# Attention, expert routing and two MLPs on one core: queries' high parts by DMA, gates through the routing matmuls

## The chip, the cores and the metric

The kernel runs on one core of a Trainium2 chip. Its metric is device time in microseconds (us). Three runs of the kernel before took 915.15, 915.86 and 917.76 us; the median is 915.86 us.

Five engines work side by side, each through its own list of instructions in a fixed order: TensorE (PE; its weight loads are PEld), VectorE (DVE), ScalarE (ACT), GpSimd (POOL) and SyncE (SP), which here only issues DMAs. An engine that waits holds up all that stands behind it in its list.

## The reference

Three layers in fp32: attention with a decay (4 batches, 8 heads, 576 rows, 64 columns), a mixture of 8 experts, and an MLP with a rational function.

```
cum    = cumsum(log(clip(f, 1e-4, 1)))                  # per head, along the 576 rows
scores = q @ k.T / 8 + cum[i] - cum[j], masked above the diagonal
attn   = exp(scores - rowmax);  attn /= attn.sum() + 1e-9
x      = attn @ v                                       # 2304 x 512 over batches and heads
logits = x @ w_gate;  e = argmax(logits)                # 8 experts
gate   = softmax(logits)[e] * sigmoid(x @ w_output_gate)[e]
y      = gate * (relu(x @ w1[e]) @ w2[e])               # 512 -> 1024 -> 512
h      = y @ w_in                                       # 512 -> 2048
out    = (P(h) / Q(h)) @ w_out                          # P cubic, Q from |h| and h*h
```

## The kernel before

Accuracy comes from splits: a number is a high part, rounded to the type that TensorE takes in one pass, and a low part, the rest. A product is three matmuls (high by high, low by high, high by low); in the scores two matmuls do it, since a second operand holds queries' high parts and rows of ones beside the low parts and the decay.

**Attention (to 198 us of the trace).** Sixteen pairs of heads are worked through, four to a batch. For each pair:

- SP loads keys `rk` and queries `rq` (64 rows of each head of the pair, 288 KB each), values `v`, and the two decay rows into `kl` (`load_c`, L387). These rows come from `cum_d` in DRAM, which the start of the kernel writes (L337) after a log (ACT L310), a running sum (DVE L314) and a split (L328, L332).
- The splits: `kh` (keys' high parts, DVE L410, two casts of 128x576 a pair), `kl` (low parts, POOL L415), `qs` high (ACT L421), `qs` low (POOL L424) and `q2s` (the copy of queries' high parts, POOL L429, function `q2h`). For the first pair DVE does the low parts and copies.
- Scores on PE (L455, L456; the last 64 rows L466, L467); the row minimum with the mask on DVE (L478, L490, function `least`); the exponential with its row sum on ACT (L510, L521); PE transposes (L573 to L593); ACT or DVE move them out of PSUM (L290, L292); the product with the values (L616) and its move out (`ot`).

After a batch's four pairs come its batch operations: sums of the last rows (`tails`, L672, L680), 1e-9 and reciprocal of the sums (`norm`, L690, L691), logits (L699 to L724), one-hot choice of the expert (`choose`, L739 to L744), the gate (`gates_a` L750 to L752, exponentials on ACT L755 and L756, `gates_b` L760 to L769), and the rows x scaled by 1/sum and gate (`rows_m` L785 on DVE, or `rows_c` L794 on ACT and `rows_g` on POOL), written to DRAM as `x_d` (L805).

The order of all that is not written by hand. `Plan` (L58) is given each operation with the engines that can do it and their lengths in ns, what it needs, buffers that it takes and frees, and a due time (`when`, in units of a pair, from the numbers `T_...`). It simulates the engines: of the operations that could begin soonest on an engine (within `NEAR` ns) it takes the one with the smallest due time; `DEAR` is a handicap of an engine where two could do the work. The result is issued in that order, and each engine keeps it.

**Routing (198 to 220 us).** With the last batch's choice, matmuls count tokens by expert (`ptot`, `pcnt`), DVE makes running sums, slots and places (L944 to L1000: counts, `ceil_div` L918 and L919, one-hot tables `so`, `rs`, `op_`), and 20 matmuls (`pid`, L1005) give each slot of an expert's tile the number of its token (`ids`, L1007). POOL gathers rows of `x_d` by `ids` (L1144). Beside it POOL scales the last batch's rows, and ACT makes the high parts of the first expert's weights (`split_unit`, L1035), DVE the low parts (L1037).

**Experts and MLP (220 us to the end).** For each of the slots' tiles: transposes (L1163), split (`hi_lo`, ACT L1063 and DVE L1064), three matmuls for each product (`mm3`, L1169 to L1171), output `ys` by ACT (L1193) to DRAM. Then the rational MLP (L1378 to L1429), which PE fills.

The lines that the change touches most, in the kernel before: the casts of the keys are DVE's alone, and the queries' second copy is POOL's.

```python
nc.vector.tensor_copy(d["kh"][:, h], d["rk"][:, h])
...
return lambda e: (nc.vector if e == "DVE" else nc.gpsimd).tensor_scalar(
    q2[half[h], h, 0:S], d["rq"][half[h], h], 1.0, 1.0, op0=ALU.mult, op1=ALU.mult
)
```

## Time and profile before

| what | value |
|---|---|
| median of three runs | 915.86 us |
| the profiled execution | 916.76 us |
| its span, first to last instruction | 915.0 us |
| PE busy | 868.4 us, 95% |
| DVE busy | 742.2 us, 81% |
| ACT busy | 619.1 us, 68% |
| POOL busy | 339.6 us, 37% |
| mean granted TensorE clock | 0.985 |

The profile is of one execution, 0.90 us above the median. 1.76 us of it lie outside the span. Busy shares are averages over stages with different limits: the stage, not the total, tells what an engine's work is worth. The clock column gives TensorE's clock as a share of its full 2.4 GHz; 0.50 is 1.2 GHz.

The span in 40 slices of 22.9 us (busy tenths) shows where PE is not full: the first slice, the seventh to ninth (137 to 206 us), and the tenth (206 to 229 us).

```
PE   6999998976799999999999999999999999999996
DVE  7798999778676689788864899989898888989873
POOL 7788595534212213223121124243332324324223
```

### The profile page before, as it was taken

Reading aid. Unit: us, or ns where it says so; the run is one execution under the profiler, and the core shown is the slowest. Engines: PE = TensorE matmul, PEld = TensorE weight load, DVE = VectorE, ACT = ScalarE, POOL = GpSimd, SP = SyncE. Lnnn points to the kernel's source line nnn. Section 1 sums busy time; section 2 is a strip of 40 time slices with the busy share of each in tenths; the row PEclk is TensorE's granted clock in tenths of the full one; section 3 lists DMA queues with packets and bytes.
Section 4 is the critical chain, followed back from the end, with each engine's and each line's share of the span. In section 5 each row is a group of like instructions: output and inputs, shape, how many; then the busy total and the mean of one; then the engine's idle time right before and its main releaser. Section 6 shows DMA issues by size and latency. Waiting matters only on the chain. (4 is left out here: it accounts for less than half of the span.)

```text
span 915.0 us, 14857 instructions
## 1 busy us (share of the span) xinstructions
PE 868.4 (95%) x4733; PEld 720.1 (79%) x4733; DVE 742.2 (81%) x1395; ACT 619.1 (68%) x1261; POOL 339.6 (37%) x356
## 2 busy tenths in 40 slices
PE   6999998976799999999999999999999999999996
PEld 5787786754688888788887778889888889988885
DVE  7798999778676689788864899989898888989873
ACT  4889887773364567666643787877676667777664
POOL 7788595534212213223121124243332324324223
PEclk9999999997999999999999999999999999999999
DMA  6675567415755378878743312011000001000001
GB/s 173 153 203 159 159 183 209 144 53 179 253 179 196 103 265 290 294 255 300 238 150 108 124 61 66 1 47 27 20 35 13 24 0 47 24 1 35 1 1 46
DMA packets 50147, 110.25 MB, mean 120 GB/s; under 512 B 8405, under 2 KB 12526, under 8 KB 50062
## 3 DMA queue, kind: packets, MB, share of 16 engines
q1 hardware_dynamic: 39214, 74.09, 26.4%
q0 software_dynamic: 10848, 35.14, 11.3%
q8 instruction: 39, 0.64, 0.3%
q14 instruction: 46, 0.38, 0.1%
HBM read 151.79 MB, written 20.35 MB: 188 GB/s over the span
## 5 line engine op out<-in xcount | busy, mean ns | idle before, releaser
L1409 POOL TENSOR_TENSOR gl<-raw,gh 128x512 fp32r<-128x512 f32 (+1 forms) x80 | 95.8, 1199 | 242.7 <-ACT gh L1408 150.2
L1425 PE MATMUL pa<-wu,gl 128*128 128x512 f32 x288 | 113.0, 392 | 1.1 <-POOL gl L1409 1.1
L1423 PE MATMUL pa<-wu,gh 128*128 128x512 f32 x288 | 113.7, 395 | 0.0
L1424 PE MATMUL pa<-wu,gh 128*128 128x512 f32 x288 | 112.6, 391 | 0.0
L1388 ACT ACTIVATE raw<-ph 128x512 f32<-128x512 f32 (+1 forms) x80 | 44.3, 553 | 80.1 <-PE ph L1380 76.8
L1064 DVE TENSOR_TENSOR colAl<-px,colAh 128x512 fp32r<-128x512 f32 x70 | 47.9, 687 | 48.7 <-ACTq L1075 25.3
L1037 DVE TENSOR_TENSOR wu<-raw,wu 128x1024 fp32r<-128x1024 f32 x64 | 75.4, 1221 | 8.4 <-ACT wu L1035 8.0
L510 ACT ACTIVATE pr<-t,mn 128x384 f32<-128x384 f32 (+3 forms) x128 | 70.6, 555 | 16.1 <-DVE mn L478 15.6
L1391 DVE SCALAR_TENSOR_TENSOR raw<-raw,babs 128x512 f32<-128x512 f32 (+1 forms) x80 | 60.8, 761 | 24.3 <-ACT raw L1389 23.8
L1401 DVE SCALAR_TENSOR_TENSOR raw<-raw,coef,raw 128x512 f32<-128x512 f32 (+1 forms) x80 | 66.0, 825 | 17.4 <-ACT raw L1397 14.4
L1378 PE MATMUL ph<-colAh,wi 128*128 128x512 f32 x192 | 74.9, 390 | 0.8 <-ACTq L1319 0.8
L1379 PE MATMUL ph<-colAl,wi 128*128 128x512 f32 x192 | 74.8, 390 | 0.2 <-DVEq L1319 0.2
L1380 PE MATMUL ph<-colAh,wi 128*128 128x512 f32 x192 | 74.7, 389 | 0.0
L1169 PE MATMUL ph<-wu,colAh 128*128 128x512 f32 x176 | 73.8, 420 | 0.7 <-ACT colAh L1063 0.7
L1169 PE MATMUL py<-wu,colAh 128*128 128x512 f32 x176 | 70.9, 403 | 1.3 <-ACT colAh L1063 1.3
L1171 PE MATMUL ph<-wu,colAl 128*128 128x512 f32 x176 | 69.8, 396 | 0.0
L1170 PE MATMUL ph<-wu,colAh 128*128 128x512 f32 x176 | 69.6, 396 | 0.0
L1171 PE MATMUL py<-wu,colAl 128*128 128x512 f32 x176 | 69.0, 392 | 0.2 <-DVE colAl L1064 0.2
L1170 PE MATMUL py<-wu,colAh 128*128 128x512 f32 x176 | 68.7, 391 | 0.0
L1063 ACT ACTIVATE colAh<-px 128x512 fp32r<-128x512 f32 x70 | 41.6, 596 | 37.4 <-PE px L1184 26.1
L1035 ACT ACTIVATE wu<-raw 128x1024 fp32r<-128x1024 f32 x64 | 63.8, 1053 | 3.2 <-DMA raw<-in_w_dram 2.8
L1425 PEld LDWEIGHTS pa<-wu,gl 128*128 128x128 f32 x288 | 54.0, 188 | 14.0 <-POOL gl L1409 2.4
(236 smaller groups left out, 2428.7 us busy)
## 6 DMA issues: line engine op xcount, KB each, us to landing
raw<-in_w_dram SPq DMA_DIRECT2D x92, 1024.0 KB
rk<-in_kT_dram SPq DMA_DIRECT2D x30, 288.0 KB
rq<-in_qT_dram SPq DMA_DIRECT2D x30, 288.0 KB
d<-in_w_in_dram POOLq DMA_DIRECT2D x16, 512.0 KB, 3.9
d<-in_w_out_dram POOLq DMA_DIRECT2D x16, 512.0 KB, 5.6
y_d<-ys SPq DMA_DIRECT2D x22, 256.0 KB
v<-in_v_dram SPq DMA_DIRECT2D x16, 256.0 KB
wo_d<-d SPq DMA_DIRECT2D x16, 256.0 KB
```

The source lines that it names most:

```text
L510: nc.scalar.activation(u["pr"][:, sl], u["t"][:, sl], AF.Exp, bias=u["mn"][:, m : m + 1], scale=-1.0, accum_out=sm[:, i, 2 * hp + h : 2 * ...
L1037: nc.vector.tensor_tensor(w[:, 1], r, w[:, 0].bitcast(F32), ALU.subtract)
L1169: nc.tensor.matmul(ps, hi[:, c, :], w[:, 0, c, :], start=start and c == 0, stop=False)
L1170: nc.tensor.matmul(ps, hi[:, c, :], w[:, 1, c, :], start=False, stop=False)
L1171: nc.tensor.matmul(ps, lo[:, c, :], w[:, 0, c, :], start=False, stop=stop and c == KD - 1)
L1378: nc.tensor.matmul(out_, wh, hi[:, :, c], start=(c == 0), stop=False)
L1379: nc.tensor.matmul(out_, wh, lo[:, :, c], start=False, stop=False)
L1380: nc.tensor.matmul(out_, wl_, hi[:, :, c], start=False, stop=(c == KD - 1))
L1409: nc.gpsimd.tensor_tensor(d["gl"], d["u_"], d["gh"].bitcast(F32), ALU.subtract)
L1423: nc.tensor.matmul(a_, gh[:, sl], wh, start=(m == 0), stop=False)
L1424: nc.tensor.matmul(a_, gh[:, sl], wl_, start=False, stop=False)
L1425: nc.tensor.matmul(a_, gl[:, sl], wh, start=False, stop=(m == MF - 1))
```

## The change

- **Plan.** New numbers `T_...`, `DEAR` and `NEAR`; a DMA's assumed latency on SP or ACT's queue is 2000 ns instead of 1000.
- **Start.** POOL's constants (zeros, ones, masks, identity) become operations of the plan, and one zeroing goes to DVE. The decay rows stay in SBUF, in a weight buffer (`cc`), instead of a trip through `cum_d`; the first pair's queries and decay rows are loaded on ACT's DMA queue.
- **Splits.** From the second pair on, `q2s` is a DMA from `qs` after its high parts are made, on SP, 30 of 147 KB, instead of 30 instructions of POOL. Casts `kh` may go to DVE or POOL, and in the first two pairs to DVE or ACT: by the order, 20 on DVE, 8 on POOL, 4 on ACT. Low parts of the first two pairs may go to DVE.
- **Batch operations.** The adds of 1e-9, the subtraction before the exponential, the gate's adds and product and the product of the gate with 1/sum go to POOL; DVE keeps a reduction (now L814) and the reciprocal (L824). The third batch's choice and gate come after the last pair.
- **Routing.** The last batch's rows are scaled by 1/sum alone, on ACT, in 40 pieces of 64 columns (L855). Its gates are not in the rows: after `ids`, five fp32 matmuls of one-hot products (`of`, L1070, by `og`) carry them to the slots (`gate`, L1076), and `ys` is scaled by it. For the other batches the same entry is 1, from the second half of `rs`, in the matmuls of `pid` (50 columns instead of 25). The rounding-up divisions become additions of a rounding constant.
- **Behind `ids`.** The low parts of the second weight unit come behind the first transposes.

The core of the diff:

```diff
-        T_BATCH, T_BATCHJ, T_ROWS = 0.299, 0.239, -5.772
...
+        T_BATCH, T_BATCHJ, T_ROWS = 0.27699, 0.20059, -5.2485
...
-        def f_store(i, t):
-            return lambda e: nc.sync.dma_start(out=cum_d[:, i, :], in_=g0[t].bitcast(F32))
...
             def load_c(e):
                 for h in range(2):
                     r = half[1 - h].start
-                    nc.sync.dma_start(out=kls[p % 2][r : r + 2, h, :].bitcast(F32), in_=cum_d[2 * p + h])
+                    queue[e].dma_start(
+                        out=kls[p % 2][r : r + 2, h, :].bitcast(F32), in_=cc[2 * p + h : 2 * p + h + 1].bitcast(F32)
+                    )
             lk, lq = {}, {}
...
+                q_ = plan.op(tl, {"SP" if p else "AQ": n}, load("rq", qT, h0, h1), takes=["rq"] if h0 == 0 else [])
                 for h in range(h0, h1):
...
+            l_c = plan.op(tl + 0.3 * SPAN, {"SP" if p else "AQ": 1200}, load_c, [o_cl, o_k[p] if p < 2 else None], takes=["c"])
...
-                    nc.vector.tensor_copy(d["kh"][:, h], d["rk"][:, h])
+                    if e == "ACT":
+                        nc.scalar.activation(d["kh"][:, h], d["rk"][:, h], AF.Copy)
+                    else:
+                        (nc.vector if e == "DVE" else nc.gpsimd).tensor_copy(d["kh"][:, h], d["rk"][:, h])
                 return go
...
             def q2h(h):
+                if p:
+                    return lambda e: nc.sync.dma_start(
+                        out=q2[half[h], h, 0:S].bitcast(F32), in_=q[half[h], h, 0:S].bitcast(F32)
+                    )
                 return lambda e: (nc.vector if e == "DVE" else nc.gpsimd).tensor_scalar(
                     q2[half[h], h, 0:S], d["rq"][half[h], h], 1.0, 1.0, op0=ALU.mult, op1=ALU.mult
...
+                khe, kle, qle, q2e = {"DVE": 520, "POOL": 1450}, {"POOL": 1480}, {"POOL": 1490}, {"SP": 1250}
+                if p < 2:
+                    khe = {"DVE": 520, "ACT": 700}
+                    kle["DVE"] = qle["DVE"] = 760
+                if p == 0:
+                    q2e = {"DVE": 850, "POOL": 1400}
+                blank_k, blank_q = (o_k[p], o_b[p]) if p < 2 else (None, None)
...
-                q2e = {"POOL": 1340} if p else {"DVE": 400}
-                o_kl.append(plan.op(w + 2, kle, kl(h), [o_kh[h]], frees=[("rk", lk[0])]))
...
-                o_q2.append(plan.op(w + 4, q2e, q2h(h), [lq[h]] + o_q2[:1], takes=["q2"] if h == 0 else [], frees=[("rq", lq[0])]))
+                o_q2.append(plan.op(w + 4, q2e, q2h(h), [o_qh[h] if p else lq[h], blank_q] + o_q2[:1], takes=["q2"] if h == 0 else [], frees=[] if p else [("rq", lq[0])]))
...
+                at = [x for x in ((slice(0, P), slice(i0, full)), (slice(0, TL), slice(NQ, i1))) if x[1].start < x[1].stop]
+                def norm_a(e, at=at):
+                    for x in at:
+                        nc.gpsimd.tensor_scalar_add(g["sums"][x], g["sums"][x], 1.0e-9)
+                def norm(e, at=at):
+                    for x in at:
+                        nc.vector.reciprocal(g["rc"][x], g["sums"][x])
+                o_n = plan.op(wn(), {"POOL": 150 * len(at)}, norm_a, need + ready + [o_mk])
+                o_n = plan.op(wn(), {"DVE": 220 * len(at)}, norm, [o_n])
+                norms.append(o_n)
                 x = {}
...
+            def gates_e(e=None):
+                nc.gpsimd.tensor_tensor(g["ex"], g["lgb"][:, :, 0:NE], g["lmax"].unsqueeze(2).to_broadcast(SH), ALU.subtract)
...
+            def gates_c(e=None):
+                nc.vector.tensor_reduce(g["den"], g["ex"], AX.X, ALU.add)
+            def gates_p(e=None):
+                den, oz = g["den"], g["oz"]
+                nc.gpsimd.tensor_scalar_add(den, den, 1.0e-9)
+                nc.gpsimd.tensor_scalar_add(oz, oz, 1.0)
+                nc.gpsimd.tensor_tensor(den, den, oz, ALU.mult)
+            def gates_r(e=None):
+                nc.vector.reciprocal(g["den"], g["den"])
+            def gates_m(e=None):
                 for r in ((slice(0, P), slice(0, NQ)), (slice(0, TL), slice(NQ, NI))):
-                    nc.vector.tensor_tensor(
-                        g["rg"][r[0], r[1], :], g["rc"][r[0], r[1], :],
-                        den[r[0], r[1]].unsqueeze(2).to_broadcast([r[0].stop, r[1].stop - r[1].start, H]), ALU.mult,
+                    nc.gpsimd.tensor_tensor(
+                        g["rg"][r], g["rc"][r], g["den"][r].unsqueeze(2).to_broadcast([r[0].stop, r[1].stop - r[1].start, H]),
...
+            def rows_a(i, y, xr):
+                np_ = P if i < NQ else TL
+                y["xr"] = xr
+                for h in range(H):
+                    sl = slice(h * D, (h + 1) * D)
+                    nc.scalar.activation(xr[:np_, sl], y["pt"][:np_, sl], AF.Identity, scale=g["rc"][:np_, i, h : h + 1])
...
+        def rows_out(i):
...
-            rows_g(i, last_y[i])
+            rows_a(i, last_y[i], wt("pr" if i < 3 else "t")[:, :DM])
...
+        nc.vector.tensor_scalar(cnt, cnt, HALF, ROUND, op0=ALU.add, op1=ALU.add)
+        nc.vector.scalar_tensor_tensor(nsl, cnt, ROUND, few, ALU.subtract, ALU.max)
+        nc.vector.tensor_tensor_scan(
+            out=send, data0=nsl, data1=zero[:, :NE], initial=0.0, op0=ALU.add, op1=ALU.add
+        )
+        nc.vector.scalar_tensor_tensor(ahead, cume[:, 0:NE], HALF, send0[:, 0:NE], ALU.add, ALU.subtract)
...
-        sidx = t_([P, NCOL], F16, name="sidx")
-        ceil_div(sidx, pos, -(P - 1) / 2)
+        sidx = t_([P, NCOL], name="sidx")
+        nc.vector.tensor_scalar_add(sidx, pos, ROUND)
         pp = t_([P, NCOL], name="pp")
-        nc.vector.scalar_tensor_tensor(pp, sidx, -float(P), pos, ALU.mult, ALU.add)
+        nc.vector.scalar_tensor_tensor(pp, sidx, ROUND, pos, ALU.subtract, ALU.subtract)
         SS = [P, NCOL, NSLOT]
-        so, rs = t_(SS, F16, name="so"), t_(SS, F16, name="rs")
...
             for c in range(c0, c0 + NI):
-                nc.tensor.matmul(pid[:, :NSLOT], op_[:, c], rs[:, c], start=(c == 0), stop=(c == NCOL - 1))
+                n = 2 if c < LAST else 1
+                nc.tensor.matmul(
+                    pid[:, : n * NSLOT], op_[:, c], rs[:, c, :n].rearrange("p a s -> p (a s)"),
+                    start=(c == 0), stop=(c == NCOL - 1), skip_group_check=True,
+                )
         ids = const.tile([P, NSLOT], I32, name="ids")
         nc.vector.tensor_scalar_add(ids, pid[:, :NSLOT], float(NT // 2))
+        den = gates_b()
+        og = t_([P, NI, NSLOT], name="og")
+        nc.vector.tensor_tensor(og, so[:, LAST:], den.unsqueeze(2).to_broadcast([P, NI, NSLOT]), ALU.mult)
+        of = ptp.tile([P, 2, NI, S], F32, tag="pT", name="of").rearrange("p h i s -> p (h i s)")[:, : NI * P]
+        of = of.rearrange("p (c q) -> p c q", q=P)
+        nc.scalar.activation(of, op_[:, LAST:], AF.Copy)
+        for i in range(NI):
+            nc.tensor.matmul(
+                pid[:, NSLOT : 2 * NSLOT], of[:, i], og[:, i], start=False, stop=(i == NI - 1), skip_group_check=True
+            )
+        gate = const.tile([P, NSLOT], F32, name="gate")
+        nc.scalar.activation(gate, pid[:, NSLOT : 2 * NSLOT], AF.Copy)
     wu_p = ctx.enter_context(tc.tile_pool(name="wu", bufs=1, reuse_waits="tile"))
...
-                nc.scalar.activation(ys, yp.pop(s), AF.Copy)
+                nc.scalar.activation(ys, yp.pop(s), AF.Identity, scale=gate[:, s : s + 1])
...
         split_unit(0, hi=False)
+        trans_x(0, col_of(0))
         split_unit(1, hi=False)
```

DVE's list at the gates of the second batch (`den` is the gate's denominator, `t` and `mn` the masked scores and their minimum, `rg` the rows' factor). Before:

```order
L752 TENSOR_REDUCE oz<-gs 128x5
L292 COPY ot<-po 128x320
L410 CAST kh<-rk 128x576
L760 TENSOR_REDUCE den<-ex 128x5
L762 TENSOR_SCALAR den<-den 128x5
L764 SCALAR_TENSOR_TENSOR den<-oz,den 128x5
L766 RECIPROCAL den<-den 128x5
L769 TENSOR_TENSOR rg<-rc,den 128x32
L769 TENSOR_TENSOR rg<-rc,den 64x8
L478 ISA t,mn<-s,mask 128x384
```

And now:

```order
L814 TENSOR_REDUCE den<-ex 128x5
L442 CAST kh<-rk 128x576
L518 ISA t,mn<-s,mask 128x512
L518 ISA mn 128x1
L442 CAST kh<-rk 128x576
L281 COPY ot<-po 128x320
L824 RECIPROCAL den<-den 128x5
```

Six instructions in a row become two that stand apart, with a row minimum (L518, L478 before), two casts and a copy between them.

The other half of that chain is now in POOL's list (L447 makes `kl`, L456 `qs` low, L819 to L828 the gate):

```order
L447 TENSOR_TENSOR kl_108<-rk,kh 64x576 x2
L456 TENSOR_TENSOR qs_104<-rq,qs_104 64x576 x2
L819 TENSOR_SCALAR den<-den 128x5
L820 TENSOR_SCALAR oz<-oz 128x5
L821 TENSOR_TENSOR den<-den,oz 128x5
L447 TENSOR_TENSOR kl_107<-rk,kh 64x576 x2
L828 TENSOR_TENSOR rg<-rc,den 128x32
L828 TENSOR_TENSOR rg<-rc,den 64x8
```

So DVE's reciprocal waits for POOL's L821, which stands behind four splits.

ACT's list at the end of routing, before (`pr`, `t`: rows of the last batch; `wu` from `raw`: high parts of the first weights; `colAh`: the first gathered rows):

```order
L755 ACTIVATE ex<-ex 128x40
L756 ACTIVATE oz<-oz 128x5
L794 ACTIVATE t<-s 64x512
L1035 ACTIVATE wu_3323<-raw_82 128x1024 x2
L1035 ACTIVATE wu_3324<-raw_83 128x1024 x2
L1035 ACTIVATE wu_3325<-raw_84 128x1024 x2
L1035 ACTIVATE wu_3326<-raw_85 128x1024 x2
L1063 ACTIVATE colAh<-px 128x512
```

And now:

```order
L855 ACTIVATE pr<-pt,rc 128x64 x15
L855 ACTIVATE t<-s,rc 64x64 x5
L803 ACTIVATE oz<-oz 128x5
L1070 ACTIVATE of<-op__3300 128x640
L1076 ACTIVATE gate<-pid 128x25
L1104 ACTIVATE wu_3354<-raw_77 128x1024 x2
L1104 ACTIVATE wu_3355<-raw_78 128x1024 x2
L1104 ACTIVATE wu_3356<-raw_79 128x1024 x2
L1104 ACTIVATE wu_3357<-raw_80 128x1024 x2
L1132 ACTIVATE colAh<-px 128x512
```

The eight weight instructions now stand behind `of`, which reads the last one-hot table, and `gate`, which reads the result of the five added matmuls.

## Rows read from the trace of the kernel before

**Rows 1.** Windows: stretch, its length, busy us (instructions) by engine, PEclk, DMA share, GB/s.

```profile
13.50:30.00 16.50, 13.36 (x76) 10.73 (x78) 10.37 (x34) 10.26 (x31) 10.11 (x21) 0.79 1.01 240
30.00:187.50 157.50, 148.48 (x1215) 120.70 (x1213) 142.63 (x477) 134.04 (x422) 108.47 (x107) 1.00 0.60 165
60.00:70.00 10.00, 10.00 (x84) 8.36 (x82) 9.27 (x34) 9.36 (x32) 9.52 (x9) 1.00 1.01 248
187.50:198.25 10.75, 10.46 (x104) 8.18 (x101) 5.94 (x28) 7.22 (x20) 2.66 (x3) 1.00 0.07 26
198.25:214.20 15.95, 3.77 (x43) 2.77 (x41) 13.86 (x38) 10.97 (x17) 8.21 (x9) 0.72 0.38 132
214.20:220.20 6.00, 4.72 (x15) 1.64 (x13) 4.67 (x5) 0.60 (x1) 4.81 (x3) 0.61 0.28 76
220.20:915.00 694.80, 680.26 (x3213) 568.98 (x3213) 555.16 (x805) 451.84 (x767) 192.96 (x185) 1.00 0.32 109
```

**Rows 2.** Timeline of the start: start, length, instruction, idle time before and releaser.

```profile
13.52 0.41 PE L456 MATMUL s<-kl,q2s 128*128 128x384 f32 x1 [4.19 <-DMA kl<-cum_d]
14.22 0.55 DVE L478 CUSTOM_DVE_ANT_0 t<-s,mask 128x384 f32<-128x384 f32 x1
```

**Rows 3.** Windows of one us each, columns as in Rows 1.

```profile
15.00:16.00 1.00, 1.00 (x6) 1.00 (x6) 0.87 (x4) 1.00 (x3) 0.18 (x2) 0.50 1.00 267
206.00:207.00 1.00, 0.00 (x0) 0.00 (x0) 0.97 (x2) 1.00 (x3) 1.00 (x2) 0.50 0.69 262
```

**Rows 4.** Timeline, 139 to 145 us.

```profile
140.58 0.26 ACT L290 ACTIVATE pT<-pt 128x128 f32<-128x128 f32 x1
142.41 1.39 POOL L424 TENSOR_TENSOR qs<-rq,qs 64x576 fp32r<-64x576 f32 x1
142.47 1.36 DVE L764 SCALAR_TENSOR_TENSOR den<-oz,den 128x5 f32<-128x5 f32 x1
144.88 0.40 PE L466 MATMUL s<-kh,qs 128*128 128x288 f32 x1 [2.60 <-DVE mn L478]
```

**Rows 5.** Lines of DVE and POOL by form, to 198.3 us: busy, mean ns, idle before.

```profile
L410 DVE CAST kh<-rk 128x576 fp32r<-128x576 f32 x32 | 21.0, 676 | 0.8 <-DMA rk<-in_kT_dram 0.8
L690 DVE TENSOR_SCALAR sums<-sums 64x8 f32<-64x8 f32 x4 | 2.9, 716 | 0.0
L764 DVE SCALAR_TENSOR_TENSOR den<-oz,den 128x5 f32<-128x5 f32 x3 | 2.7, 905 | 0.3
L429 POOL TENSOR_SCALAR q2s<-rq 64x576 fp32r<-64x576 f32 x30 | 20.3, 678 | 2.0
```

**Rows 6.** Timeline of DVE in routing.

```profile
202.63 0.20 DVE L760 TENSOR_REDUCE den<-ex 128x5 f32<-128x40 f32 x1 [1.12 <-ACT ex L755]
203.28 0.17 DVE L764 SCALAR_TENSOR_TENSOR den<-oz,den 128x5 f32<-128x5 f32 x1
204.37 1.05 DVE L979 TENSOR_TENSOR pos<-pos,oh 128x160 f32<-128x160 f32 x1
206.39 0.96 DVE L918 TENSOR_SCALAR quot<-pos 128x20 f32<-128x20 f32 x1
208.39 0.97 DVE L988 SCALAR_TENSOR_TENSOR pp<-sidx,pos 128x20 f32<-128x20 f16 x1
214.00 0.19 DVE L1007 TENSOR_SCALAR ids<-pid 128x25 int32<-128x25 f32 x1 [0.40 <-PE pid L1005]
```

**Rows 7.** Timeline of POOL, ACT and PE in routing.

```profile
204.04 3.28 POOL L785 TENSOR_TENSOR pr<-pr,rg 128x512 f32<-128x512 f32 x3 [1.42 <-DVE rg L769]
203.07 7.68 ACT L1035 ACTIVATE wu<-raw 128x1024 fp32r<-128x1024 f32 x8
213.81 4.43 PE L1256 MATMUL ph<-h 128*128 128x512 bf16 x10
219.53 0.60 ACT L1063 ACTIVATE colAh<-px 128x512 fp32r<-128x512 f32 x1 [8.79 <-PE px L1163]
220.18 0.50 PE L1169 MATMUL ph<-wu,colAh 128*128 128x512 f32 x1 [0.69 <-ACT colAh L1063]
```

More of the change, by code (lines that the diff above doesn't have):

```diff
@@ L34 @@
 }
-DEAR = {"ACT": 45.9, "DVE": 316.0}
-NEAR = 108.2
+DEAR = {"ACT": 55.495, "DVE": 310.925}
+NEAR = 14.997
 WARM = 6830
@@ L53, in reaches @@
     def reaches(self, engine):
[L54 removed]
+        lat = 2000 if self.engine in ("SP", "AQ") else LATENCY.get((self.engine, engine), 200)
         return self.end + lat
@@ L295, in evac_len, with c_blank, go, c_keys @@
             return {"ACT": 60 + 0.836 * n, "DVE": 85 + 1.04 * n}
+        queue = {"SP": nc.sync, "AQ": nc.scalar}
+        early = -4 * SPAN
+        def c_blank(i):
+            def go(e):
+                nc.gpsimd.memset(q2s[i].bitcast(F32), 0.0)
+                for h in range(2):
+                    nc.gpsimd.memset(q2s[i].bitcast(F32)[half[1 - h].start : half[1 - h].start + 2, h, 0:S], 1.0)
+            return go
+        def c_keys(i):
+            return lambda e: (nc.vector if e == "DVE" else nc.gpsimd).memset(kls[i].bitcast(F32), 0.0)
+        def c_masks(e):
+            nc.gpsimd.memset(mask, 0.0)
+            nc.gpsimd.memset(mask_t, 0.0)
+            for t in [mask[:, (NQ - 1) * P :]] + [mask_t[h * TL : (h + 1) * TL, S // 2 - TL :] for h in range(2)]:
+                nc.gpsimd.affine_select(
+                    out=t, in_=t, compare_op=ALU.is_ge, fill=BIG / SCALE, base=0, pattern=[[-1, t.shape[-1]]],
+                    channel_multiplier=1,
+                )
+        def c_gaps(e):
+            for t in qs:
+                nc.gpsimd.memset(t.bitcast(F32)[:, :, S:], 0.0)
+            make_identity(nc, identf)
+        def c_rest(e):
+            for t in vs:
+                nc.gpsimd.memset(t[: P - TL, :, NQ], 0.0)
+            nc.gpsimd.iota(
+                pref, pattern=[[-1, NE]], base=NE, channel_multiplier=0, allow_small_or_imprecise_dtypes=True
+            )
+            nc.gpsimd.tensor_copy(prefs, pref.unsqueeze(1).to_broadcast([P, NI, NE]))
+            nc.gpsimd.memset(prefs[TL:, NQ], 0.0)
+        o_k = [plan.op(early, {"DVE": 1050}, c_keys(0))]
+        o_b = [plan.op(early, {"POOL": 3200}, c_blank(0))]
+        o_m = plan.op(early + 2, {"POOL": 2300}, c_masks, o_b[:1])
+        o_g = plan.op(early + 3, {"POOL": 1300}, c_gaps, [o_m])
+        o_k.append(plan.op(early + 4, {"POOL": 1100}, c_keys(1), [o_g]))
+        o_b.append(plan.op(early + 4, {"POOL": 2700}, c_blank(1), [o_g]))
+        o_r = plan.op(early + 5, {"POOL": 1800}, c_rest, [o_b[1]])
         g0 = {}
@@ L685, in batch @@
                     need = [plan.op(wn(), {"DVE": 150}, tails2, [a2], frees=[("pt", a2)])]
-                def norm(e, i0=i0, i1=i1, full=full):
-                    for rs_, sl in ((slice(0, P), slice(i0, full)), (slice(0, TL), slice(NQ, i1))):
-                        if sl.start < sl.stop:
-                            nc.vector.tensor_scalar_add(g["sums"][rs_, sl, :], g["sums"][rs_, sl, :], 1.0e-9)
-                            nc.vector.reciprocal(g["rc"][rs_, sl, :], g["sums"][rs_, sl, :])
-                o_n = plan.op(wn(), {"DVE": 250 * (2 if i1 == NI else 1)}, norm, need + ready + [o_mk])
+                at = [x for x in ((slice(0, P), slice(i0, full)), (slice(0, TL), slice(NQ, i1))) if x[1].start < x[1].stop]
[8 more added lines that the diff above has]
+                norms.append(o_n)
                 x = {}
@@ L910, in tile_attention_moe_mlp @@
         nc.gpsimd.memset(zero, 0.0)
+        few = t_([P, NE], name="few")
+        nc.gpsimd.memset(few, 0.0)
+        nc.gpsimd.memset(few[:, 0:1], 1.0)
         SH = [P, NE, NCOL]
[L913 to L924 removed]
+        for i in range(2):
+            rows_out(i)
         vector_order = rctx.enter_context(tc.manual_schedule(engines={mybir.EngineType.DVE}))
@@ L931, in tile_attention_moe_mlp @@
         nc.tensor.matmul(pcnt[:, :NEC], after, ohf, start=True, stop=True)
+        gates_e()
         gates_a()
+        for i in range(2, NI):
+            rows_out(i)
         gates_x()
-        for i in range(3, NI):
-            rows_copy(i)
         incl, pos3 = t_(SH, name="incl"), t_(SH, name="pos3")
@@ L969, in tile_attention_moe_mlp @@
-        counting = count()
-        for _ in range(3):
-            next(counting)
-        for _ in gates_b():
-            next(counting, None)
-        for _ in counting:
-            pass
-        for i in range(NI):
-            rows_out(i)
-        nc.vector.tensor_tensor(pos3, pos3, base.unsqueeze(2).to_broadcast(SH), ALU.add)
+        ahead = const.tile([P, NE], F32, name="ahead")
+        HALF = (P - 1) / (2.0 * P)
+        nc.vector.tensor_tensor_scan(
+            out=incl.rearrange("p e c -> p (e c)"), data0=ptot[:, :NEC], data1=zero, initial=0.0,
+            op0=ALU.add, op1=ALU.add,
+        )
```

226 lines of the change are left out of this document (88 added, 138 removed).

## The prediction, made before the changed kernel ran

> **What bounds the kernel now.** I read the totals first (TensorE 95% busy), then windows, since an average hides where the 5% lie. [rows 1] cut the span where PE's work changes. From 220.2 us on PE is busy 680.26 of 694.80 us at full clock, and the change alters none of its 3213 instructions there: that stretch is worth nothing. In a good stretch of attention, 60 to 70 us, PE is busy 10.00 of 10.00, so a faster VectorE or GpSimd buys nothing there either. What can be won or lost lies in four places: 13.5 to 30 us (idle 16.50 − 13.36 = 3.1 us, and at a mean clock of 0.79 another 0.21 x 16.5 = 3.4); 30 to 187.5 us (157.5 − 148.48 = 9.0 us idle); the tail after the last row minimum (10.75 us); and routing, from the last row maximum to the first expert matmul, 15.95 + 6.00 us in which PE does little that matters. Next I read the waits inside these places in the timelines, and last, for what the edits remove, the sums by line.
>
> **Part A, the start.** PE's second score matmul waits 4.19 us for the decay rows to come through DRAM, begins at 13.52, and the first row minimum runs at 14.22 [rows 2]. The clock then stands at 0.50, 1.2 GHz, with PE fully busy, behind that idle stretch [rows 3]. The change drops the trip through DRAM. But in the new order ACT issues four loads of queries ahead of the first exponent-side work, the log comes after them, and DVE does splits of the second pair ahead of the first minimum. I estimate that the first minimum stays at 14 to 15 us, and that the gain comes afterwards: the second pair is already split when PE wants it, so the later idle stretch and the second fall of the clock go. That is about half of the 6.5 us: −3.0. Bounds: 0 (log and scan late by what the DRAM trip took) and −6.
>
> **Part B, the attention loop.** 9.0 us idle [rows 1]. The largest single wait is at the gates of a batch: PE's L466 waits 2.60 us for a row minimum [rows 4]. Ahead of that minimum stood DVE's chain of six small instructions, one of which, L764 on 128x5, ran 1.36 us, from 142.47, while POOL's L424 ran 1.39 us from 142.41. Alone the same instruction takes 0.17 us [rows 4, 6]; its mean in three batches is 0.905 [rows 5]. So DVE pays there for running beside POOL. Taking such instructions to POOL removes that: three gate chains at about 2.3 us of adds and products, the 1e-9 adds (2.9 us in four of one form alone), and 12 of 32 casts at 0.676 = 8.1 us [rows 5]. Only what PE waits for counts, which is at most the 9.0. I take −5.0: the two stalls of over 2 us at gates, as at 144.88, go in full, and a little of the rest. Bounds 0 and −9; beyond 0 is the third rival.
>
> What is added there: POOL loses 30 copies at 0.678 = 20.3 us [rows 5] and gains 8 casts (between 0.68 and 1.44 us each by L429 and L424, so at most 11.5) and some 50 small ones; it has 49 us free in 157.5 [rows 1]: hidden. The copies become 30 DMAs of 147 KB, 4.4 MB. At 248 GB/s, what the DMA engines moved when full [rows 1], that is 18 us of 157.5, and takes their share from 0.60 to 0.71: hidden on average. A single copy of 147 KB may stand behind a load of 1 MB, 4.2 us at 248 GB/s, and its buffer comes free with the last score of the pair but one; between that and the first score that needs it lie 85 to 110 matmuls in either order, about 10 us at 84 matmuls in 10 us. So it isn't late, by some 5 us. If that cover went, PE would wait for it at every pair.
>
> **Part C, the tail.** 10.75 us from the last minimum to the last batch's maximum [rows 1]. The third batch's choice and gate now stand in it, some 12 small DVE instructions of 0.2 us in a stretch where DVE is busy 5.94 us of 10.75. Most hide: +0.8, bounds −1 and +2.
>
> **Part D, routing up to ids.** 198.25 to 214.00 us, 15.75 us, nearly all DVE, one instruction behind the other. Gone is the gate chain with its wait of 1.12 us for ACT, 0.20 + 1.12 + four instructions of 0.15 to 0.19 between the counts, net 1.9 us. Gone are one ceil-division step and the addition of an offset, 0.3 at their undisturbed price. The rest is price: instructions on 128x20 run 0.96 or 0.97 us (three of them, the first and last in [rows 6]) beside POOL's products [rows 7], while 128x5 and 128x8 alone take 0.17. In all they lose about 4.0 us to POOL: 3 x 0.8 at L918 to L988, 0.7 at L979, and an estimated 0.8 at a copy and an add of like size. If POOL did nothing: −6.2. It does: the third batch's five products now fall here in place of seven, so 5/7 of 4.0 = 2.8 comes back. I take −3.4. Bounds −6.2 and 0.
>
> The rows show that a small DVE instruction ends with the POOL instruction beside it: 1.36 us for 0.17. The Trainium skill says of the SBUF ports (SBUF — State Buffer, "Who interferes with whom") that DVE instructions with two SBUF inputs contend with a GpSimd instruction that reads SBUF, and that the other engine is blocked for the whole instruction. By it all five products would hold DVE for up to a full length each, and the term would be −2.0 instead of −3.4.
>
> **Part E, ids to the first expert matmul.** 214.00 to 220.18 = 6.18 us before [rows 6, 7]. ACT's eight weight splits, 7.68 us from 203.07, were over long before [rows 7]. In the new list they stand behind `of`, which needs the last one-hot table, and `gate`, which needs the five added matmuls, which need `og`, behind `ids` and four gate instructions on DVE. `colAh`, which the first matmul needs, stands behind the eight. So: four gate instructions and og, 1.3 (4 x 0.2 and one of 128x125); five matmuls 0.7 (0.25 to 2.0; a 128x288 one takes 0.40 [rows 4]); gate 0.25 (L290's 128x128 takes 0.26); eight splits 7.68; colAh 0.60; sum 10.6. That is **+4.4**, rounded to +4.5 for the hand-overs. Bounds +3.1 (og 0.7 and matmuls 0.25) and +6.3 (matmuls 2.0, og held by POOL).
>
> ACT's own work before it hides: 40 pieces of 64 columns at no more than 0.26 (the 128-column row of [rows 4]) are 10.4 us against 3.0 for five whole rows; they run from 198.5 to about 209, while `of` can begin at about 210. If a piece took 0.35 they would push it by 3.
>
> **Part F, the clock.** PE idles for some 4 us between the ten idle matmuls (4.43 us behind `ids` [rows 7]) and the first expert matmul. In routing the clock went from 1.00 to 0.50 some 4 us after PE had stopped [rows 1, 3]. So the experts may start at 1.2 GHz: about 3.6 us at half clock cost 1.8. I take +1.0.
>
> The Trainium skill (TensorE: Matmul & The Clock Gate, "HAM oscillation — how this bites in real kernels") describes just this, a wait after which the next work starts cold. By it the term would be the whole 1.8.
>
> Hidden: the scale in `ys`, 22 times on ACT, which has 243 us free in its stretch [rows 1].
>
> **Sum.** −3.0 − 5.0 + 0.8 − 3.4 + 4.5 + 1.0 = −5.1 against the profiled execution's 916.76: 911.7. That execution lies 0.90 above the median of the runs, so the median of the new kernel comes to **910.8 us**.
>
> **Rivals.**
>
> *Larger gain.* The idle 9.0 us go whole, 5 at the start, routing runs at −6.2, and the clock stays up: −9.0 − 5.0 + 0.8 − 6.2 + 4.5 = −14.9, or 901.0. For it: every stall over 2 us that I found is of one kind, DVE late. Against it: there is always a next one, and the idle part of many short waits is not DVE's alone.
>
> *Nothing.* A and B give 2 to 3 us each less, since POOL's answer takes the place of DVE's chain: about 915.9. For it: in the new order DVE's reciprocal waits for POOL's product, which stands behind splits of 1.4 us.
>
> *Slower.* The same round trip, at its worst: DVE's reciprocals (about nine that fall in the loop) each wait out one POOL split of 1.44 us (L424's mean, 1.39 in [rows 4]), with row minima queued behind them, and half of it reaches PE: +6.5. Of the relief of part B only 1.5 is left, so B becomes +5.0, and the sum is −3.0 + 5.0 + 0.8 − 3.4 + 4.5 + 1.0 = +4.9: 915.86 + 4.9 = 920.8, about 921. The other parts sum to −0.1, so it decides as soon as half of nine waits exceeds that 1.5: at a mean wait of a reciprocal for POOL of 0.35 us. For it: POOL is busy 69% of the loop [rows 1]. Against it: the copies are off POOL's list, and the reductions come well ahead of the reciprocals.
>
> *The copies by DMA come late.* Each of 15 pairs waits, say, 1 us: 15 us, above 920. The 10 us of cover speak against it; its chance is within the slower case.
>
> **How the numbers follow.** Forecast 0.52 (its own range 906 to 914.5), larger gain 0.16, nothing 0.16, slower 0.16. The range 901 to 918.5 leaves out half of the slower case and a little of the largest gain. What a measurement can tell from no change is 0.3%, 2.7 us. Faster: the larger gain, and most of the forecast's own cases (0.47): 0.63. Same: the nothing case and what is left of the forecast's upper end: 0.21. Slower: 0.16.
>
> **What would show it.** Right: from ids to the first expert matmul about 10.7 us, with ACT's eight splits right before `colAh`; routing up to ids about 12.4; the wait of 2.6 us at the gates gone; PE idle in the loop about 4 us. Wrong: waits of DVE's reciprocals for POOL above 0.35 us in the mean, PE waiting for `q2s`; ACT's eight splits done before `ids`; or a first minimum later than 16 us.

## The result

The changed kernel takes 923.53 us (median of four runs, 922.38 to 923.9); the kernel before 916.8 (four runs, the three of the start among them). The ratio is 1.0068, 95% interval 1.0049 to 1.0087: slower by 0.7%. Forecast were 910.8, a range of 901 to 918.5, and "faster". The profiled execution has a span of 922.0 us against 915.0.

Where the 7.0 us lie, by five instants of the two traces:

| stretch | before | after | difference | forecast |
|---|---|---|---|---|
| start to first row minimum | 14.22 | 16.74 | +2.5 | parts A and B |
| first to last row minimum | 173.28 | 170.48 | −2.8 | together −8.0 |
| last row minimum to last row maximum | 10.75 | 13.57 | +2.8 | +0.8 |
| row maximum to `ids` | 15.75 | 14.34 | −1.4 | −3.4 |
| `ids` to first expert matmul | 6.18 | 12.16 | +6.0 | +4.4 |
| from there to the end | 694.8 | 694.7 | −0.1 | +1.0 (clock) |

So the price of the tail of routing came true and more, and the gain that was to pay for it in attention did not come. Against the forecast, 12.1 us are missing: 7.7 in parts A and B together, 2.0 in C, 2.0 in D, 1.5 in E (against its rounded +4.5), and F was 1.1 better. The windows of the changed kernel answer to [rows 1] (stretch, length, busy us and instructions of PE, PEld, DVE, ACT, POOL, then PEclk, DMA share, GB/s):

```profile
4.00:16.00 12.00, 4.46 (x61) 3.92 (x59) 7.01 (x10) 5.81 (x10) 11.25 (x23) 0.82 1.03 237
30.00:187.00 157.00, 148.06 (x1199) 119.45 (x1199) 125.36 (x432) 131.15 (x417) 96.44 (x107) 0.99 0.73 191
187.22:200.79 13.57, 12.83 (x121) 8.68 (x118) 8.65 (x34) 8.08 (x24) 1.91 (x8) 1.00 0.00 1
200.79:215.13 14.34, 4.87 (x43) 3.36 (x42) 13.35 (x27) 9.13 (x41) 5.72 (x8) 0.69 0.47 165
215.13:227.29 12.16, 6.84 (x24) 3.97 (x25) 3.49 (x9) 8.67 (x11) 6.49 (x7) 0.64 0.27 75
227.29:922.00 694.71, 680.67 (x3213) 569.97 (x3213) 557.58 (x808) 453.27 (x767) 190.41 (x182) 0.99 0.32 108
```

In the loop VectorE is relieved, about 142 to 125 us, GpSimd too, 108 to 96, and PE is as idle as before: 157.00 − 148.06 = 8.9 us. What rose is the DMA share, 0.60 to 0.73, and at the start it is full where it was not: in the kernel before it was 0.58 in the same twelve us:

```profile
4.00:16.00 12.00, 7.81 (x74) 7.29 (x72) 10.21 (x17) 3.38 (x7) 10.70 (x29) 0.92 0.58 159
```

PE's waits in the loop, 30 to 187 us, have new names (who, for whom: us, times, longest):

```profile
PE pt L633 <- DVE xr L843: 2.8, 1, 2.8
PE s L496 <- DMA q2s<-qs: 2.1, 2, 1.7
```

The timeline shows what is behind the first: VectorE itself waited 3.23 us for a row buffer, whose last content a DMA had yet to write out.

```profile
165.56 0.69 DVE L843 TENSOR_TENSOR xr<-pt,rg 128x512 f32<-128x512 f32 x1 [3.23 <-DMA x_d<-xr]
166.31 0.66 PE L633 MATMUL pt<-identf,pr 128*128 128x128 f32 x4 [2.85 <-DVE xr L843]
```

There are three row buffers, and the write of the first row went out on GpSimd's queue at 159.42; the buffer was free some 6 us later. From 154 to 166 us the DMA share is 0.96 to 1.20. A weight load of 1 MB, issued at 156.45, is part of that, beside the loads and the copies; how much of this wait is the copies' own isn't shown.

By the profile's releasers, the two late copies are those issued 10.8 and 10.1 us ahead of the matmuls that waited for them, the first right behind another weight load of 1 MB:

```profile
129.97 0.59 SPq L905 DMA_DIRECT2D raw<-in_w_dram  x1
130.66 0.52 SPq L462 DMA_DIRECT2D q2s<-qs  x1
133.91 0.55 SPq L462 DMA_DIRECT2D q2s<-qs  x1
141.49 0.44 PE L496 MATMUL s<-kl,q2s 128*128 128x384 f32 x1 [0.39 <-DMA q2s<-qs]
144.05 0.41 PE L496 MATMUL s<-kl,q2s 128*128 128x384 f32 x1 [1.72 <-DMA q2s<-qs]
```

So the cover of about 10 us that the prediction counted on was there at this place, and the copies needed all of it, where 4.2 us had been allowed for.

Behind the wait for `q2s` and its neighbours (PE idle 2.06 of the 4 us from 140) the clock fell, 0.60 from 144 to 148 us, which costs 1.6 us by that clock. The stall of 2.60 us at the gates [rows 4], for which the change was made, is gone.

Routing and what follows, timelines of the changed kernel, VectorE, GpSimd, ScalarE and PE:

```profile
201.26 3.34 DVE L788 TENSOR_TENSOR sc<-sc,prefs 128x40 f32<-128x40 f32 x1
207.45 1.07 DVE L1027 TENSOR_TENSOR pos<-pos,ahead 128x160 f32<-128x160 f32 x1
208.55 1.04 DVE L1028 TENSOR_TENSOR pos<-pos,oh 128x160 f32<-128x160 f32 x1
215.13 0.18 DVE L1063 TENSOR_SCALAR ids<-pid 128x25 int32<-128x25 f32 x1 [0.41 <-PE pid L1058]
```

```profile
201.50 3.04 POOL L843 TENSOR_TENSOR xr<-xr,rg 128x512 f32<-128x512 f32 x3
207.29 2.12 POOL L843 TENSOR_TENSOR xr<-xr,rg 128x512 f32<-128x512 f32 x2 [2.75 <-ACT xr L860]
219.02 0.52 POOL L1320 MEMSET h<- 128x512 f32 x1 [9.61 <-PE pid L1072]
220.14 1.10 POOL L1214 DMA_INDIRECT xg<-x_d,ids  x1 [0.60 <-issue]
```

```profile
214.76 0.74 ACT L1070 ACTIVATE of<-op__3300 128x640 f32<-128x640 f16 x1 [2.79 <-DVE op__3300 L1051]
218.93 0.19 ACT L1076 ACTIVATE gate<-pid 128x25 f32<-128x25 f32 x1 [3.44 <-PE pid L1072]
219.07 7.68 ACT L1104 ACTIVATE wu<-raw 128x1024 fp32r<-128x1024 f32 x8
226.66 0.57 ACT L1132 ACTIVATE colAh<-px 128x512 fp32r<-128x512 f32 x1
```

```profile
216.59 2.30 PE L1072 MATMUL pid<-og,of 128*128 128x25 f32 x10 [1.50 <-DVE og L1067]
223.72 0.63 PE L1233 MATMUL px<-identf,xg 128*128 128x128 f32 x4
227.29 0.80 PE L1239 MATMUL ph<-wu,colAh 128*128 128x512 f32 x1 [2.94 <-ACT colAh L1132]
```

L788, 0.20 us in the kernel before, ends with GpSimd's third product in a row. The eight splits, at 203.07 before [rows 7], begin at 219.07, behind `gate`. And one thing that the prediction did not have: GpSimd's memset and the gathers wait for the added matmuls as well, 5.0 us behind `ids`, against 0.5 before.

### The profile page after: what moved, and what is told of

It is laid out like the page before. It is cut to its first block, busy times and chain, and to the rows that moved or that the text cites. A ratio compares the mean times of both kernels' runs of the same rounds, so it can differ in the third digit from the quotient of the medians.

```text
span 922.0 us, 14973 instructions
## 1 busy us (share of the span) xinstructions
PE 873.3 (95%) x4742; PEld 723.0 (78%) x4743; DVE 728.1 (79%) x1354; ACT 628.5 (68%) x1302; POOL 320.7 (35%) x358
## 5 line engine op out<-in xcount | busy, mean ns | idle before, releaser
L550 ACT ACTIVATE pr<-t,mn 128x128 f32<-128x128 f32 (+3 forms) x128 | 70.6, 556 | 9.4 <-DVE mn L518 9.2
L518 DVE CUSTOM_DVE_ANT_0 t<-s,mask 128x384 f32<-128x384 f32 (+3 forms) x128 | 57.9, 485 | 15.1 <-PE s L496 9.7
```

Source lines behind the costliest of these rows:

```text
L550: nc.scalar.activation(u["pr"][:, sl], u["t"][:, sl], AF.Exp, bias=u["mn"][:, m : m + 1], scale=-1.0, accum_out=sm[:, i, 2 * hp + h : 2 * ...
```

## The experiments

Times are medians; each is compared with runs of the kernel before on the same chip (917.88, 917.58, 917.42 and 918.75 us in the four groups; 916.8 beside the changed kernel), so differences between groups are good to a us or two. e_splits, e_gather and e_norows ran once each and have no interval. Stages are read from each run's own trace. Seven traces have the changed order up to the last row maximum (the changed kernel, e_splits, e_gather, e_both, e_norows, e_v1, e_wk1): the maximum comes at 197.74 to 200.79 us, in the middle 198.73, so the changed kernel's own trace is the latest of them, and attention as a whole is about level with 198.25 before.

**From ids to the experts.** Three edits, alone and together; the third, not shown here, issues the three gathers ahead of the memset of the idle tile:

```diff
-        nc.scalar.activation(of, op_[:, LAST:], AF.Copy)
+        nc.gpsimd.tensor_copy(of, op_[:, LAST:])
-        nc.scalar.activation(gate, pid[:, NSLOT : 2 * NSLOT], AF.Copy)
+        nc.vector.tensor_copy(gate, pid[:, NSLOT : 2 * NSLOT])
```

> The changed kernel with two operations moved off ScalarE: GpSimd makes the table `of`, VectorE copies `gate`; the eight weight splits then follow the row pieces. In the changed kernel ids to the first expert matmul took 12.16 us. Theory Q (ScalarE's list is all of the loss): back to about 6.5 us, the whole kernel 5.7 us faster. Theory M (two chains of like length: ScalarE's list, and GpSimd's memset that waits for the five added matmuls and holds the gathers behind it): the first rows still land at 223.7 on the scale of the changed kernel, the first expert matmul begins some 1.4 us later, 9.9 us behind ids, 2.2 us faster.

> The changed kernel with the first three gathers issued ahead of the memset of the idle tile, nothing else. Theory Q and theory M: the gather begins within 0.6 us of ids (in the changed kernel 5.0 us behind), yet the first expert matmul doesn't move by more than 0.3 us, since it waits for ScalarE's eight splits until 226.66. If ScalarE's list were not the bound, it would come up to 3.5 us sooner.

> Both edits together: `of` and `gate` off ScalarE, gathers ahead of the memset. Theory Q: the same as the first edit alone, about 6.5 us from ids to the first expert matmul. Theory M: only both together bring it there, to 5.5 to 6.5 us from ids, the kernel 5.7 to 6.6 us faster than the changed one, about 917.5, level with the kernel before.

Measured, e_splits (edit above): 918.12 us, `ids` 211.59, first expert matmul 222.26, so 10.67 us, 1.5 less: theory M, within 0.8 us of its figure; Q's 6.5 is out. The total is better by more than that because `ids` came 3.5 us sooner in this run, which the edit can't have caused. e_gather (gathers written ahead of the memset): 924.74 us, 14.99 from `ids`, 2.8 *more*. e_both: 924.61 us (ratio 1.0083, 1.0056 to 1.0109), 15.81. Both were forecast wrong, by theory M too. The trace of e_both, GpSimd, shows why:

```profile
217.22 2.10 POOL L1214 DMA_INDIRECT xg<-x_d,ids  x1 [4.17 <-DVE gate L1076]
221.85 0.54 POOL L1322 MEMSET h<- 128x512 f32 x1
```

The gather, though first in its list, still began 4.6 us behind `ids` (212.60), and then the memset, the idle matmuls and, in PE's list behind these, the transposes of the gathered rows were late. The next two runs asked what holds it.

```diff
# e_v1 and e_wk1, each with one of the two lines for `of`, and with the three edits above
-        of = ptp.tile([P, 2, NI, S], F32, tag="pT", name="of").rearrange("p h i s -> p (h i s)")[:, : NI * P]
-        of = of.rearrange("p (c q) -> p c q", q=P)
+        of = vs[1].rearrange("p a i d -> p (a i d)").rearrange("p (c q) -> p c q", q=P)   # e_v1
+        of = t_([P, NI, P], name="of")                                                    # e_wk1
...
-        warm(10)
+        warm(1)
```

> The changed kernel with `of` and `gate` off ScalarE, gathers ahead of the memset, `of` placed in the buffer of an old value tile instead of the table's, and one idle matmul instead of ten. Theory N: in the runs before, the gather could begin only behind the five added matmuls (PE's 2.30 us, 3.8 us behind ids), since the rows' buffers reuse the memory that `of` stood in. Then here the gather begins within 0.6 us of ids, the first expert matmul 6.0 to 7.5 us behind ids (12.16 in the changed kernel, 14.99 and 15.81 in the last two runs with gathers first), and the kernel takes about 917. Rival O: what holds the gather is the closing of the routing stage as a whole, whatever memory `of` has; then the gather still begins 4.2 us behind ids or later, and the first expert matmul some 9.5 to 10 us behind ids, since only the nine idle matmuls are gone.

> The changed kernel with the edits of the run before (`of` and `gate` off ScalarE, gathers ahead of the memset, one idle matmul), but `of` in a tile of its own among the work tiles, whose memory neither the weight splits nor the rows' buffers reuse. Theory N (memory that the added matmuls read holds what is put there next: the gathers when it is the table's, ScalarE's splits when it is a value tile's): the gather begins within 1 us of ids, the splits before ids, and the first expert matmul 6.0 to 7.5 us behind ids, against 12.16; the kernel 4.5 to 6 us faster than the changed one, about 918. Rival O (closing the routing stage holds them whatever memory is read): 11 us or more as in all four runs so far.

e_v1: 922.93 us; the gather began 0.84 us behind `ids`, as theory N says, but the first expert matmul 12.07 us behind it: now ScalarE's splits waited until 216.88, behind the matmuls (214.49 to 216.79). The profile names no releaser for them, but in e_wk1, which differs in the place of `of` alone, they begin at 209.39: the weights' buffer reuses the value tile's memory. e_wk1, where neither the gathers nor the splits wait, takes 7.18 us from `ids`. Its ScalarE and PE:

```profile
209.39 7.75 ACT L1103 ACTIVATE wu<-raw 128x1024 fp32r<-128x1024 f32 x8
219.25 0.60 ACT L1131 ACTIVATE colAh<-px 128x512 fp32r<-128x512 f32 x1 [2.11 <-PE px L1232]
219.90 0.79 PE L1238 MATMUL ph<-wu,colAh 128*128 128x512 f32 x1 [0.75 <-ACT colAh L1131]
```

The kernel takes 919.19 us, ratio 1.0025 (0.9994 to 1.0055): 5.0 us of the stage are back (nine idle matmuls fewer have a part in that, which isn't told apart), and it can no longer be told from the kernel before; its ten runs lie between 913.73 and 926.63. That the memory of `of` decides who waits is shown by the three places: two held what next uses their memory, the third nothing. Rival O falls.

**GpSimd beside VectorE in routing.**

```diff
             def rows_g(i, y):
-                scaled(i, y, nc.gpsimd, y["xr"])
+                pass
```

> The changed kernel without GpSimd's five products of the third batch's rows (the rows are written unscaled; left out of the computation). Theory P (VectorE's small two-input instructions are held while GpSimd computes): L788, 3.34 us, falls to 0.20 and L1027, L1028, 1.07 and 1.04, to about 0.32 each; last row maximum to ids falls from 14.34 to about 9.8 us. Rival (they are slow from DMA writes or from ScalarE's pieces): those three stay within 0.3 us, and the stretch stays at 14 us.

918.99 us; row maximum to `ids` 9.87 us, 4.5 less; L788 0.34, L1027 0.33, L1028 0.32. Theory P, to 0.1 us: five products of GpSimd, 5.2 us together, cost VectorE 4.5. In this order the first three fall on L788 and the other two on L1027 and L1028.

**The attention loop.**

```diff
# e_q2pool: the queries' copies on GpSimd again, in the changed kernel
-                khe, kle, qle, q2e = {"DVE": 520, "POOL": 1450}, {"POOL": 1480}, {"POOL": 1490}, {"SP": 1250}
+                khe, kle, qle, q2e = {"DVE": 520, "POOL": 1450}, {"POOL": 1480}, {"POOL": 1490}, {"POOL": 1340}
...
# b_q2dma: the DMA alone, in the kernel before
             def q2h(h):
+                if p:
+                    return lambda e: nc.sync.dma_start(
+                        out=q2[half[h], h, 0:S].bitcast(F32), in_=q[half[h], h, 0:S].bitcast(F32)
+                    )
...
-                q2e = {"POOL": 1340} if p else {"DVE": 400}
+                q2e = {"SP": 1250} if p else {"DVE": 400}
...
```

> The changed kernel with the copies of queries' high parts back on GpSimd, from the second pair on; the planner orders the rest anew. Theory D (copies by DMA cost more than they free: PE waited 2.1 us for q2s and 2.8 for a row buffer that a full DMA queue held, and the clock fell once behind it, 1.6): DMA share from 30 to 187 us falls from 0.73 to about 0.62, both waits are gone, last row maximum 3 to 6 us earlier, kernel about 919. Rival G (GpSimd becomes the bound again, 30 copies of 0.68 us): GpSimd's busy time in that stretch rises from 96 to about 112 us and the last maximum comes no earlier or later: kernel 923 or more.

> The kernel before with one part of the change alone: queries' high parts copied by DMA from the second pair on. Theory D (the DMA copies are what costs the attention loop): DMA share from 30 to 187 us rises from 0.60 to about 0.7, PE waits for q2s, row buffers or loads, the last row maximum comes 3 to 8 us later, the kernel at 921 to 926. Rival (it was the new order of the run without them, not the DMA): within 2 us of 917.6.

e_q2pool: **913.88 us**, ratio 0.9960 (0.9941 to 0.9980): 0.4% faster than the kernel before, and 9.6 us below the changed one (1.1% by the two ratios), more than theory D said. The last maximum comes at 195.98. In its loop PE is idle 3.3 us instead of 8.9, at full clock, though GpSimd is as busy as rival G feared:

```profile
30.00:187.00 157.00, 153.74 (x1251) 122.77 (x1251) 135.38 (x460) 135.35 (x431) 112.24 (x133) 1.00 0.63 166
```

Half of the gain lies elsewhere: row maximum to `ids` is 9.73 us, since the third batch's products came out before the maximum in this order (the last ends at 194.45), and L788 takes 0.20. That part is the order's and not the copies'. b_q2dma: 934.81 us, ratio 1.0178 (1.0159 to 1.0197), beyond theory D's range: PE waits 3.7 us for `q2s`, but longer for ScalarE's exponentials (5.9), the DMA share from 30 to 187 us is 0.74, and the last maximum comes at 218.04. The planner, told of other engines, ordered everything anew, still with 1000 ns as a DMA's latency, and how much of the 17 us is order isn't told apart.

All traces together bound what is shown. PE waits for `q2s`, 0.4 to 4.3 us from 30 us on, in ten of the eleven traces with copies by DMA, and in none of those with copies on GpSimd. But PE's idle time from 30 to 187 us is 6.1 to 8.9 us in the changed order, 9.4 to 12.6 in the four other orders with copies by DMA, and with copies on GpSimd 9.0 (the kernel before), 3.3 (e_q2pool, and f_q2wk1 below in the same order) and 8.9 (f_start2 below; f_start is left out). Copies off DMA end that wait; the 3.3 us needed this order as well, and no run has the copies moved in a fixed order.

> The changed kernel's operations ordered with the due times, DEAR and NEAR of the kernel before. Theory T (the new numbers fit the new operations): last row maximum 2 us or more later, kernel 925 or more. Rival (the numbers are worth nothing on the chip, what the planner gains is lost to waits that it doesn't know): within 1.5 us of 923.5, either way.

932.41 us, ratio 1.0159 (1.0133 to 1.0186): the changed operations with the numbers of the kernel before are 9 us slower than with their own. Theory T: the new numbers are worth something for the new operations. So each run that changes what the planner is told carries a part for the order, of the size of the effects sought; e_q2pool got faster with such a part in it, and it may be luck that its order is a good one.

**The start.**

> The changed kernel with casts of the first two pairs' keys on VectorE alone, and the split of the decay sums (L362, which stood behind two casts of ScalarE that wait for loads, 9.01 us) ahead of the second split of queries. Theory S (ScalarE's list made the start late): L362 at about 5.9 us, decay rows landed at about 11, the first row minimum at 12.5 to 14.0 (16.1 to 17.0 in the five runs of the changed order), and the last row maximum 2 to 3 us earlier, the kernel about 921. Rival: the DMA queues are full in these 16 us (share 0.90), the decay rows wait there for loads of later pairs: the first minimum stays above 15.5, the kernel at 923.

> The same with the second pair's loads held until the decay sums are split. Theory L (at the start the DMA queues are full with loads of later pairs, so casts and decay rows wait): first row minimum at 13 to 15 us instead of 16.1 to 17.7, last row maximum about 2 us earlier, kernel about 906.5. Rival (the second pair is late instead, PE idles at about 20 us as it did in the kernel before): no gain, 908 to 910.

> The changed kernel with the first pair's decay rows on SyncE's queue and every later pair's loads of keys and queries behind them in it (in the run before, the planner had only put a later pair in the second's place, and the DMA share from 4 to 16 us stayed full). Theory L (full DMA queues make the start late): DMA share from 4 to 12 us well below 1.0, the split of the decay sums ahead of 8 us, first row minimum at 12 to 14.5 us instead of 16.1 to 17.7; what comes of it by the last row maximum depends on the second pair, then loaded from about 9 us: up to 2 us earlier. Rival (the order of the engines alone makes it late): first minimum above 15.5.

e_log (keys' casts on VectorE, the decay sums' split second in ScalarE's list): 928.28 us, L362 at 8.68, first minimum 17.66: the running sum now stood behind a cast of VectorE that waited 3.71 us for its load, so L362 came 0.3 us earlier instead of 3.1. Its numbers failed, but theory S itself was hardly put to the test. f_start (f_q2wk1, described below, with the second pair's loads held): 996.08 us; it doesn't compute the kernel's output, so its time stands for nothing. The loads did not move and the DMA share from 4 to 16 us stayed at 1.03 to 1.05, so it tells nothing of theory L either. e_start2 put the decay rows ahead of all later pairs' loads in SyncE's list:

```diff
-            l_c = plan.op(tl + 0.3 * SPAN, {"SP" if p else "AQ": 1200}, load_c, [o_cl, o_k[p] if p < 2 else None], takes=["c"])
+            l_c = plan.op(tl + 0.3 * SPAN, {"SP": 1200}, load_c, [o_cl, o_k[p] if p < 2 else None], takes=["c"])
...
-                k = plan.op(tl, {"SP": n}, load("rk", kT, h0, h1), takes=["rk"] if h0 == 0 else [])
-                q_ = plan.op(tl, {"SP" if p else "AQ": n}, load("rq", qT, h0, h1), takes=["rq"] if h0 == 0 else [])
+                k = plan.op(tl, {"SP": n}, load("rk", kT, h0, h1), [st[0]["l_c"]] if p else [], takes=["rk"] if h0 == 0 else [])
+                q_ = plan.op(tl, {"SP" if p else "AQ": n}, load("rq", qT, h0, h1), [st[0]["l_c"]] if p else [], takes=["rq"] if h0 == 0 else [])
```

934.92 us, ratio 1.0166 (1.0125 to 1.0208). DMA share 0.82, 0.00 and 0.22 in the three stretches of 4 us from 4 us on, first minimum 14.96, between the two forecasts: the full queues held it by 1.8 of the 2.5 us (1.1 to 2.0 against the seven traces). L362 came at 8.95 all the same, so the rest may be the order of the lists. The last maximum comes at 216.99: PE is idle 2.8 us from 16 to 30 and 12.0 us from 30 to 187, and how much of that is the late second pair and how much the new order isn't told apart.

**Putting together what helped.**

> The changed kernel with copies on GpSimd again (913.88 by itself) and the mended way from ids to the experts. If both causes are independent, 913.9 minus 4.5 to 6: about 908 to 909.5. If the second only uncovers another wait, 912 or more.

> The same start with the copies on GpSimd and the mended way to the experts (910.76 by itself). If the start's 2 us reach the end: 908 to 909. If the second pair is late instead (PE idle at about 20 us, as in the kernel before): 910 to 913.

f_q2wk1: **910.76 us**, ratio 0.9920 (0.9903 to 0.9936), faster than both kernels. It lies between the two forecasts. From `ids` to the experts 7.17 us instead of 12.18, but only 3.1 of the 5.0 us reach the end. In its trace, of an execution 2.05 us above the median, the expert stage is 4 us longer than in e_q2pool's: PE waits 3.3 us for a transposed index table in both, and here the clock fell behind it (0.57 and 0.58 below):

```profile
238.00:242.00 4.00, 2.59 (x7) 2.14 (x8) 2.71 (x10) 0.00 (x0) 0.54 (x1) 0.57 0.54 164
242.00:246.00 4.00, 4.00 (x14) 3.13 (x14) 0.00 (x0) 0.93 (x2) 0.09 (x1) 0.58 0.07 27
```

f_start2: 923.58 us (ratio 1.0057, 1.0034 to 1.0081), first minimum 15.21, last maximum 206.88 instead of 195.55, and 13 us more than f_q2wk1 in all. PE waits 2.5 us for the second pair's queries, until 25.29. The rest is in the order: PE is idle 8.9 us from 30 to 187 instead of 3.3, and GpSimd's five products of the third batch fall behind the last maximum again (L788 takes 3.34 us, row maximum to `ids` 14.40 instead of 9.72). What the early loads of the changed kernel are worth by themselves isn't shown.

## Why the prediction was wrong, point by point

- **Part B, the attention loop, and in it the copies by DMA: the step that failed.** In idle time part B's −5.0 became −0.1: 8.9 us instead of 9.0. The stalls at the gates went, and waits that the prediction had put at nothing came in their place: 2.8 us for a row buffer that DMA had yet to write out, 2.1 us for `q2s`, and 1.6 us of clock behind it. "Hidden on average", a share of 0.71, was right as an average (0.73 measured). What was mis-sized is a copy's way through the queues: 4.2 us behind a load of 1 MB, and so "it isn't late, by some 5 us", where two copies took about 10 us, behind such a load and others. And it wasn't asked who else waits there: the row writes. The rival "the copies by DMA come late" was named, at 1 us in each pair; it came in one pair, with 2.1 us.
- **What the copies cost in all stays open.** Taking them back gave 9.6 us in the changed kernel, of which 4.6 lie behind the last row maximum and come from the order; adding them cost 17 in the kernel before, with more waits for exponentials than for copies. Both runs were ordered anew.
- **Part B's gain was there to be had in one order.** e_q2pool, which keeps GpSimd's share of the batch work, is idle 5.7 us less in the loop than the kernel before (−5.0 forecast). The rival of slow round trips over GpSimd isn't what happened: no wait of VectorE for GpSimd shows in the changed kernel's loop.
- **Part A, −3.0 forecast, +2.5 at the first minimum, put at 14 to 15 us.** A part of it is full DMA queues, overlooked here as well. That the second pair is ready early was right: PE is idle 1.0 us from 16 to 30 us, against 3.1, and the second fall of the clock (0.55 from 24 to 27 us before) is gone.
- **Part C, +0.8 forecast, +2.8 measured**, outside its bounds. PE does 121 instructions there instead of 104 [rows 1] and is busy 12.83 of the 13.57 us: the term left out what the order leaves for PE.
- **Part D, −3.4 forecast, −1.4 measured**, inside its bounds. The five products cost 4.5 us, not 2.8: e_norows. The rule of the Trainium skill (SBUF — State Buffer, "Who interferes with whom"), a whole length of the other's instruction, gave −2.0 and was the better price. The trace agrees that an instruction is held whole lengths, and L788 was held for three of them in a row.
- **Part E, +4.4 forecast, +6.0 measured**, inside its bounds of +6.3. The mechanism, splits behind `gate`, is right, but half of the story: e_splits, without it, still took 10.67 us, since memory that the added matmuls read held the gathers. The mis-sized term is the matmuls, 2.30 us instead of 0.7 (ten records of 0.23).
- **Part F** was half right: the experts began at 1.2 GHz (0.50 until 230 us), against 1.00 before, yet the stage to the end is as long as before; what made up for it isn't shown.

## What to carry to other kernels

A copy moved from an engine to DMA is not free because the queues have room on average: ask when its source is ready, what stands ahead of it in the queue at that moment, and who else waits for a transfer there. Work put at a joint of two stages was paid twice here, once in the engine lists and once in memory that the next stage reuses; where such a buffer lies decided which engine stood still. And when a planner makes the order, an edit of its operations also changes the order, by amounts like those sought: to price one edit, hold the order fixed, or say that it isn't priced.

## What the runs showed of the hardware

- A VectorE instruction of 0.20 us was held for 3.34 us by three GpSimd products in a row, not by one: it did not get in between them.
- With the DMA share at 1.03 (12 to 16 us), two transfers of 4.5 KB issued from 10.71 us on ScalarE's queue released their matmul only at 16.05; in the kernel before (0.59), two issued from 12.03 on SyncE's queue released it at 13.52.
- Two copies of 144 KB, issued at 130.66 and 133.91 us, were waited for until 141.49 and 144.05.
- An idle stretch of PE of 3.3 us at the same place was followed by a clock of 0.58 (242 to 246 us) in f_q2wk1, by a shorter fall in e_q2pool (0.91 over the 20 us around it), and by none in e_wk1 (1.00).
